# A windowed-attention and expert-attention kernel rewritten: block transposes on VectorE, packed TensorE tiles, expert pairs woven into the next batch

## The chip, the cores and the metric

One Trainium2 chip, one core of it. The metric is the time of one execution in device microseconds (us), the median of several runs. A core has TensorE (PE in the profile; its weight loads are PEld), VectorE (DVE), ScalarE (ACT), GpSimd (POOL) and SyncE (SP), which here only issues transfers.

## The reference, cut to what matters

```python
# q, k, v: (8 batches, 8 heads, 576, 64), float32
scores = matmul(q, k.T) / 8;  mask = abs(i - j) <= 32     # windowed attention
attn = exp(scores - max) * mask; attn /= attn.sum(-1)
x = (attn @ v) as (8, 576, 512)                           # heads side by side
logits = x @ w_gate                                       # 4 experts, the best 2 kept, softmax of the 2
for e in range(4):
    q, k, v = x @ wq[e], x @ wk[e], x @ wv[e]             # 512 -> 64
    a = softmax(causal(q @ k.T / 8))                      # 576 x 576
    out += weight[e] * (a @ v @ wo[e])                    # 64 -> 512
```

The largest score is not subtracted in either kernel; the inputs are small.

## The kernel before, in words

All loops are unrolled when the program is built, and a scheduler of the framework orders each engine's instructions by priority (the order of the source) and readiness; waits and buffers follow from tiles and pools.

For each batch the windowed attention goes head by head. `stage_qk_dma` (L126) loads q (SP queue) and k (ACT queue) in blocks of 128 positions; `stage_qk_compute` (L146) transposes each block for two heads on TensorE (L151) and ACT (L155) and DVE (L157) copy the results out. `head_stage1` (L165) loads v beside a column block of ones (L169, L171), makes the scores of five key blocks, each against the queries that its band reaches (L188, 832 columns a head, contraction over the 64 features of the head), lets ACT take the exponential (L193, L195, L200) and POOL multiply by the band mask (L202, L208, L210). `head_stage2` (L215) multiplies by v and the ones (L230), adds the overlapping edges of the blocks (L240 to L245), takes the reciprocal of 64x576 sums on DVE (L248) and multiplies (L249) into `XTF`, x transposed. Every float32 matmul shows in the trace as two load-and-multiply pairs.

`moe_batch` (L252) casts x to bfloat16 (L255), makes the gate in float32 (L262) and its top-2 weights on DVE, projects (L310, L321), and then goes through four experts one after the other: scores of one key block (L339), exponential (L361), triangle mask on DVE (L363), product with v and ones (L368), reciprocal and weight per block of queries (L390 to L394), transposes (L399). Last come the output projection with a contraction over 64 (L407), the copy (L410) and the store (L411). PSUM is a rotation of 8 single banks.

The order of the source is heads(0), then for each b: heads(b+1), moe(b). The loads for batch b+2 are issued among the heads of b.

Of the kernel before, what the change touches and what calls it, by code (L numbers as in the profile page):

```python
# [8 lines left out]
F32 = mybir.dt.float32  # L10
# [4 lines left out]
SUB = mybir.AluOpType.subtract  # L15
IS_GE = mybir.AluOpType.is_ge
AXX = mybir.AxisListType.X


@with_exitstack  # L20
def kernel(
# [12 lines left out]
    nc = tc.nc  # L34
    B, H, S, D = q.shape
    assert D == 64
    E, DM, HD = moe_wq.shape
    assert HD == 64 and DM == H * D and E == 4
    assert S % 128 == 64 and S == 576, "kernel tuned for S=576"
    W = 32  # L40
# [4 lines left out]
    NTB = (S + 127) // 128  # L45
    NKB = NTB
    NQT = NTB
    NKT = NTB

    kblocks = []  # L50
    for kb in range(NKB):
        k0 = 128 * kb
        nk = min(128, S - k0)
        q_lo = max(0, k0 - W)
        q_hi = min(S, k0 + nk + W)
        kblocks.append((k0, nk, q_lo, q_hi - q_lo))
    at_off = []
    acc = 0
    for (_, _, _, qw) in kblocks:
        at_off.append(acc)  # L60
        acc += qw
    ATW = acc

    consts = ctx.enter_context(tc.tile_pool(name="consts", bufs=1))
    wpool = ctx.enter_context(tc.tile_pool(name="wpool", bufs=1))
    stage = ctx.enter_context(tc.tile_pool(name="stage", bufs=1))
    natp = ctx.enter_context(tc.tile_pool(name="natp", bufs=12))
    qkt = ctx.enter_context(tc.tile_pool(name="qkt", bufs=3))
    vwp = ctx.enter_context(tc.tile_pool(name="vwp", bufs=3))
    atp = ctx.enter_context(tc.tile_pool(name="atp", bufs=3))  # L70
    xwp = ctx.enter_context(tc.tile_pool(name="xwp", bufs=2))
    xtp = ctx.enter_context(tc.tile_pool(name="xtp", bufs=2))
    mpool = ctx.enter_context(tc.tile_pool(name="mpool", bufs=2))
    smallp = ctx.enter_context(tc.tile_pool(name="smallp", bufs=2))
    psum = ctx.enter_context(tc.tile_pool(name="psum", bufs=1, space=bass.MemoryType.PSUM))

    def psum_b1(name):
        return psum.tile([128, 512], F32, name=name, tag="B1", bufs=8)
# [5 lines left out]
    BMK = consts.tile([128, 192], F32, name="BMK")  # L84
    nc.vector.memset(BMK, 1.0)
    nc.gpsimd.affine_select(BMK, BMK, pattern=[[1, 192]], compare_op=IS_GE, fill=0.0,
                            base=0, channel_multiplier=-1)
    nc.gpsimd.affine_select(BMK, BMK, pattern=[[-1, 192]], compare_op=IS_GE, fill=0.0,
                            base=64, channel_multiplier=1)
    QW0 = kblocks[0][3]  # L90
    BMK0 = consts.tile([128, QW0], F32, name="BMK0")
    nc.vector.memset(BMK0, 1.0)
    nc.gpsimd.affine_select(BMK0, BMK0, pattern=[[1, QW0]], compare_op=IS_GE, fill=0.0,
                            base=32, channel_multiplier=-1)
    nc.gpsimd.affine_select(BMK0, BMK0, pattern=[[-1, QW0]], compare_op=IS_GE, fill=0.0,
                            base=32, channel_multiplier=1)
    MT = consts.tile([128, 128], BF16, name="MT")
    nc.vector.memset(MT, 1.0)
    nc.gpsimd.affine_select(MT, MT, pattern=[[1, 128]], compare_op=IS_GE, fill=0.0,
                            base=0, channel_multiplier=-1)  # L100

    WG = wpool.tile([128, NDT, 4], F32, name="WG")
    nc.sync.dma_start(WG[:, :, :], moe_w_gate.rearrange("(t p) e -> p t e", p=128))
    WQP = [wpool.tile([128, NDT, 128], BF16, name=f"WQP{j}") for j in range(2)]
    WKP = [wpool.tile([128, NDT, 128], BF16, name=f"WKP{j}") for j in range(2)]
    WV = wpool.tile([128, NDT, 4 * 64], BF16, name="WV")
    WO = wpool.tile([64, E, DM], BF16, name="WO")
# [368 lines left out]
```

## Time and profile before

| what | us |
|---|---|
| timed runs | 916.01, 922.34, 925.95 |
| median | 922.34 |
| span of the profiled execution, first to last instruction | 916.9 |
| TensorE / VectorE / ScalarE / GpSimd busy in it | 744.7 / 504.8 / 317.1 / 174.6 |

The profiled execution is known by its span alone; what lies around the span is not in its record. Busy shares are means over the whole span; matmul ends are modelled, so neighbouring matmuls overlap in their records. PEclk is the granted TensorE clock in tenths or as a fraction of 2.4 GHz: the two levels are 1.0 (2.4 GHz) and 0.5 (1.2 GHz).

### The profile page before, as it was taken

The page shows a single profiled execution, that of the slowest core. Times are in us where ns is not written, and L with a number is a line of the kernel's source. Part 1 is how long each engine was busy: PE and PEld are TensorE (multiplying, and loading weights), DVE is VectorE, ACT ScalarE, POOL GpSimd, SP SyncE. Part 2 cuts the span into 40 slices and gives each one's busy share as a digit, 9 for nine tenths or more (in the row PEclk, how much of TensorE's full clock was granted, in tenths as well). Part 3 has the DMA queues.
Part 4 walks back from the last instruction along what each step waited for, and adds up shares of the span by engine and source line. Part 5 has one row for each costly group of instructions (what it writes and reads, how often), then busy time and mean ns, then how long its engine had stood idle before and what let it go on. Part 6 is the DMA issues. An engine that isn't in the chain of part 4 may idle for free.

```text
span 916.9 us, 10477 instructions
## 1 busy us (share of the span) xinstructions
PE 744.7 (81%) x3328; PEld 482.0 (53%) x3328; DVE 504.8 (55%) x1410; ACT 317.1 (35%) x1009; POOL 174.6 (19%) x267
## 2 busy tenths in 40 slices
PE   1798967859898598976979679895899679974997
PEld 1576735524675256743558435672467435852552
DVE  2328567672556716477174761658608960598242
ACT  1334333333423324233243233432424333333243
POOL 1044511001520014200242002420036002500000
PEclk9998656755757557575576755776559655776575
DMA  9936123001330013200141001110012001100001
GB/s 180 196 77 134 28 51 72 20 0 47 73 69 20 0 46 86 63 13 1 46 94 39 7 0 46 26 33 0 1 51 49 4 1 46 39 1 1 35 18 53
DMA packets 126407, 40.54 MB, mean 44 GB/s; under 512 B 121488, under 2 KB 121488, under 8 KB 126352
## 3 DMA queue, kind: packets, MB, share of 16 engines
q1 hardware_dynamic: 83728, 29.38, 13.7%
q10 hardware_dynamic: 42624, 10.49, 6.0%
q8 instruction: 27, 0.44, 0.2%
q14 instruction: 28, 0.23, 0.1%
HBM read 30.42 MB, written 9.44 MB: 43 GB/s over the span
## 4 chain that ended last, share of the span: by engine, by line
PE 66%; DVE 23%; DMA 4%; ACT 3%; issue 2%; ACTq 1%; SPq 0%; DVEq 0%
DVE REC L248 15%; PE pSB L188 10%; PE pOB L230 9%; PE py L407 8%; PE po L368 7%; PE pOA L230 7%; PE pSA L188 7%; PE pst L339 6%; PE pg L262 4%; PE pp L310 4%; PE ptt L399 3%; DVE XTF L249 3%; PE ptq L151 2%; DMA nat<-in_k_dram 2%; DVE XW L243 2%
## 5 line engine op out<-in xcount | busy, mean ns | idle before, releaser
L248 DVE RECIPROCAL REC<-XW 64x576 f32<-64x576 f32 x64 | 239.9, 3748 | 10.9 <-ACT XW L245 8.9
L368 PE MATMUL po<-VE,ATE 128*128 128x65 bf16 (+2 forms) x480 | 79.6, 245 | 69.5 <-DVE ATE L363 39.4
L151 PE MATMUL ptq<-ident,nat 128*128 128x128 f32 (+1 forms) x320 | 77.9, 376 | 62.2 <-DMA nat<-in_q_dram 18.5
L202 POOL TENSOR_TENSOR ATK<-ATK,BMK 128x160 f32<-128x160 f32 x64 | 34.3, 536 | 429.4 <-ACT ATK L193 428.4
L368 PEld LDWEIGHTS <-ATE 128*128 128x128 bf16 (+2 forms) x480 | 43.9, 117 | 126.0 <-ACT XTB L255 40.7
L188 PE MATMUL pSB<-QT,KT 64*128 64x192 f32 (+1 forms) x384 | 103.5, 404 | 2.4 <-ACT ATK L193 2.4
L230 PE MATMUL pOB<-ATK,VWK 128*128 128x192 f32 (+1 forms) x384 | 100.2, 392 | 0.8 <-ACT XW L245 0.8
L361 ACT ACTIVATE ATE<-pst 128x512 bf16<-128x512 f32 (+2 forms) x192 | 70.3, 390 | 85.9 <-PE pst L339 64.0
L208 POOL TENSOR_TENSOR ATK<-ATK,BMK 128x576 f32<-128x576 f32 x64 | 89.7, 1402 | 48.2 <-ACT ATK L195 45.7
L151 PEld LDWEIGHTS ptq<-ident,nat 128*128 128x128 f32 (+1 forms) x320 | 48.4, 183 | 91.3 <-DVE KT L157 25.2
L243 DVE TENSOR_TENSOR XW<-XW,pOA 128x64 f32<-128x64 f32 x64 | 14.0, 219 | 147.2 <-ACT XW L240 146.5
L188 PEld LDWEIGHTS pSB<-QT,KT 64*128 64x128 f32 (+1 forms) x384 | 80.3, 235 | 26.3 <-issue 22.0
L230 PEld LDWEIGHTS pOB<-ATK,VWK 128*128 128x128 f32 (+1 forms) x384 | 82.5, 242 | 21.2 <-issue 12.7
L243 DVE TENSOR_TENSOR XW<-XW,pOB 128x64 f32<-128x64 f32 x192 | 41.4, 220 | 94.1 <-ACT XW L245 86.7
L188 PE MATMUL pSA<-QT,KT 64*128 64x160 f32 (+1 forms) x256 | 78.9, 447 | 0.0
L407 PE MATMUL py<-WO,OTT 64*128 64x512 bf16 (+1 forms) x160 | 77.5, 623 | 0.0
L230 PE MATMUL pOA<-ATK,VWK 128*128 128x160 f32 (+1 forms) x256 | 73.0, 420 | 4.3 <-issue 1.4
L339 PE MATMUL pst<-QE,KE 64*128 64x512 bf16 (+2 forms) x192 | 69.1, 387 | 2.3 <-ACT ATE L361 2.3
L245 ACT COPY XW<-pOB 128x128 f32<-128x128 f32 (+1 forms) x192 | 45.2, 242 | 72.5 <-DVE XW L243 51.4
L390 DVE RECIPROCAL rr<-po 128x1 f32<-128x1 f32 (+1 forms) x160 | 26.3, 165 | 64.3 <-PE po L368 63.9
L193 ACT ACTIVATE ATK<-pSA 128x352 f32<-128x352 f32 x64 | 29.7, 465 | 84.1 <-PE pSA L188 76.7
L188 PEld LDWEIGHTS pSA<-QT,KT 64*128 64x128 f32 x256 | 54.4, 268 | 8.4 <-issue 8.2
(70 smaller groups left out, 858.3 us busy)
## 6 DMA issues: line engine op xcount, KB each, us to landing
nat<-in_k_dram ACTq DMA_DIRECT2D x32, 256.0 KB, 4.5
nat<-in_q_dram SPq DMA_DIRECT2D x32, 256.0 KB, 4.3
VWK<-in_v_dram SPq DMA_DIRECT2D x64, 128.0 KB, 2.3
out_dram<-ysb SPq DMA_DIRECT2D x32, 256.0 KB, 2.0
VWK<-in_v_dram ACTq DMA_DIRECT2D x64, 16.0 KB, 2.4
nat<-in_q_dram SPq DMA_DIRECT2D x8, 128.0 KB, 3.0
nat<-in_k_dram ACTq DMA_DIRECT2D x8, 128.0 KB, 3.7
out_dram<-ysb SPq DMA_DIRECT2D x8, 128.0 KB, 2.3
```

Of the source, the lines that this page charges most:

```text
L151: nc.tensor.transpose(pt[:, 0:nt], nat[:nt, 2 * g:2 * g + 2, :].rearrange("p h d -> p (h d)"), ident[:nt, :nt])
L188: nc.tensor.matmul(tgt[0:nk, col:col + qw], KTl[g][pofs:pofs + 64, k0:k0 + nk], QTl[g][pofs:pofs + 64, q_lo:q_lo + qw], start=True, stop=True)
L208: nc.gpsimd.tensor_tensor(out=a13, in0=a13, in1=BMK[:, None, 0:iw].to_broadcast([128, 3, iw]), op=MULT)
L230: nc.tensor.matmul(tgt[:, col:col + qw], VWK[0:nk, kb, :], ATK[0:nk, at_off[kb]:at_off[kb] + qw], start=True, stop=True)
L243: nc.vector.tensor_tensor(out=XW[:, q_lo:prev_hi], in0=XW[:, q_lo:prev_hi], in1=tgt[:, col:col + ovl], op=ADD)
L245: nc.scalar.copy(XW[:, prev_hi:q_hi], tgt[:, col + ovl:col + qw])
L248: nc.vector.reciprocal(REC[0:64, :], XW[64:128, :])
L262: nc.tensor.matmul(pg[0:nt, 4 * tb:4 * tb + 4], XTF[dt][:, t0:t0 + nt], WG[:, dt, :], start=(dt == 0), stop=(dt == NDT - 1))
L339: nc.tensor.matmul(pst[0:nkk, 0:cw], KE[jj2][eo2:eo2 + 64, k0:k0 + nkk], QE[jj2][eo2:eo2 + 64, k0 + c:k0 + c + cw], start=True, stop=True)
L361: nc.scalar.activation(ATE[0:nkk, c:c + cw], pst[0:nkk, 0:cw], EXP, scale=scale_moe)
L368: nc.tensor.matmul(po[qt][0:nq, 0:65], ATE[0:nkk, q0 - k0:q0 - k0 + nq], VE[kt][0:nkk, e, 0:65], start=(kt == 0), stop=(kt == qt))
L407: nc.tensor.matmul(py[0:nq, 0:DM], OTT[:, e, q0:q0 + nq], WO[:, e, :], start=(e == 0), stop=(e == E - 1))
```

## The change

Nearly everything is rewritten; inputs, outputs and types (float32 for the windowed part and the gate, bfloat16 for the experts) stay. The windowed attention takes 4 heads at a time (g = 0, 1). q and k of four heads are loaded so that each head fills 32 partitions, and four VectorE transposes of 32x32 blocks (two halves of the 64 features each for q and k) replace the TensorE transposes. Each score matmul contracts over 32 partitions into 64 partitions of PSUM, and the two feature halves accumulate: a head, a feature half and the parity of the 64-wide key block give a part of the array of its own. The sums of the four heads come from matmuls with one-hot columns into 32 partitions each, 128x144 in all, and one reciprocal serves them. v multiplies in segments whose 128 keys cover the band of the segment, so nothing is added at edges; the reciprocals are spread over partitions by a matmul with a selector (`rb`). v is loaded once for a batch, and two SBUF-to-SBUF transfers make the blocks that begin at odd multiples of 64.

The experts go in pairs: scores of both into one two-bank tile, one exponential for up to 1024 elements of a partition, triangle masks by POOL, one set of normalizing instructions per pair, and the output projection contracts over both experts (128). PSUM is 4 slots of two banks. Of batch b-1, gate, projections and scores stand among the heads of batch b. All transfers but the weights go through the SP queue, q and k of the first batch first.

```diff
-    (stage_qk_dma, stage_qk_compute, head_stage1, head_stage2, moe_batch)
+    natp bufs=3; qkt, vp, xp, mp, atep bufs=2; atp, yp bufs=3; psum bufs=4 of [128, 2, 512] f32
+    def load_qk(b, g):
+        for nm, src in (("qn", q), ("kn", k)):
+            t = natp.tile([128, 18, 64], F32, name=nm, tag=nm)
+            for hh in range(4):
+                nc.sync.dma_start(t[32 * hh:32 * hh + 32, :, :],
+                                  src[b, 4 * g + hh].rearrange("(tb p) d -> p tb d", p=32))
+    def load_v(b):
+        t = vp.tile([128, 8, H, 64], F32, name="vsb", tag="vsb")
...
+        pairs = t[:, :, :, :].rearrange("p (m o) h d -> p m o (h d)", o=2)
+        nc.sync.dma_start(pairs[64:128, :, 1, :], pairs[64:128, :, 0, :])
+        nc.sync.dma_start(pairs[0:64, 0:3, 1, :], pairs[0:64, 1:4, 0, :])
+    EBLK = [[(0, 0, 96), (1, 96, 224), (2, 224, 288)], [(2, 288, 352), (3, 352, 480), (4, 480, 576)]]
+    OBLK = [[(0, 0, 160), (1, 160, 288)], [(2, 288, 416), (3, 416, 576)]]
+    SEGS = [(0, 96), (96, 160), (160, 224), (224, 288), (288, 352), (352, 416), (416, 480), (480, 576)]
+    def win_scores(b, g):
+        for T, nm in ((KT, "kn"), (QT, "qn")):
+            for dh in range(2):
+                nc.vector.transpose(T[:, dh, :].rearrange("p (t x) -> p t x", x=32),
+                                    n_[:, :, 32 * dh:32 * dh + 32])
+        for half in range(2):
+            sl = [slot("sc0"), slot("sc1")]
+            with tc.manual_schedule(engines={PE}):
+                for s in range(3):
+                    for dh in range(2):
+                        for par, blk in ((0, eb), (1, ob)):
...
+                            for hh in range(4):
+                                r = slice(32 * hh, 32 * hh + 32)
+                                nc.tensor.matmul(
+                                    sl[hh // 2][64 * par:64 * par + 64, hh % 2, lo - c0:hi - c0],
+                                    KT[r, dh, k0:k0 + 64], QT[r, dh, lo:hi],
+                                    start=(dh == 0), stop=(dh == 1), skip_group_check=True)
+            for p in range(2):
+                nc.scalar.activation(ap, sl[p][:, :, 0:HS], EXP, scale=scale_att)
+                nc.gpsimd.tensor_tensor(out=ap, in0=ap, in1=MASK[...], op=MULT)   # 128 x 576
+    def win_out(b, g):
+        ss = slot("sums")
+        for hh in range(4):
+            for j in range(4):
+                nc.tensor.matmul(ss[32 * j:32 * j + 32, 0, 0:144], OH[:, hh, :],
+                                 A[:, hh, 144 * j:144 * j + 144], ...)
+        nc.vector.reciprocal(R, ss[:, 0, 0:144])
+        for pair in range(2):
+                for c, (lo, hi) in enumerate(SEGS):
+                    for x in range(2):
+                        nc.tensor.matmul(up_[64 * x:64 * x + 64, half, ...], V[:, c, 4 * g + hh, :], A[:, hh, lo:hi], ...)
+        for pair in range(2):
+            nc.scalar.copy(us, u[pair][:, :, 0:HS])
+            for j in range(4):
+                nc.tensor.matmul(rb[...144 columns], SEL[:, j, pair, :], R, start=True, stop=True)
+            nc.vector.tensor_tensor(out=XTF[...], in0=us, in1=rb[:, :, 0:HS], op=MULT)
+            nc.gpsimd.tensor_copy(XTB[:, dt, :], XTF[:, dt, :])
+    moe_scores(b, j): 12 matmuls of the two experts j, 4 exponentials (3 of 1024, 1 of 128 elements), 4 affine_select on POOL
+    moe_av(b, j): 30 matmuls, 2 x (reciprocal, weight, scale), 5 transposes of both experts, 1 copy
+    moe_y(b): 10 matmuls of 512 columns, copies of 1024 on DVE, ACT, DVE, 3 stores
+    load_weights()
+    for b in range(B + 1):
+        for g in range(2):
+            if b + 1 < B:
+                load_qk(b + 1, g)
+                if g == 0:
+                    load_v(b + 1)
+            if b < B:
+                win_scores(b, g)
+            if b > 0:
+                if g == 0:
+                    moe_gate(b - 1); moe_proj_qk(b - 1, 0); moe_scores(b - 1, 0); moe_proj_v(b - 1)
+                else:
+                    moe_av(b - 1, 0)
+            if b < B:
+                win_out(b, g)
+            if b > 0:
+                if g == 0:
+                    moe_proj_qk(b - 1, 1); moe_scores(b - 1, 1)
+                else:
+                    moe_av(b - 1, 1); moe_y(b - 1)
```

## Rows read from the trace of the kernel before

**Rows 1.** The page: busy time of each engine, and the granted clock by slice.
```profile
PE 744.7 (81%) x3328; PEld 482.0 (53%) x3328; DVE 504.8 (55%) x1410; ACT 317.1 (35%) x1009; POOL 174.6 (19%) x267
...
PEclk9998656755757557575576755776559655776575
```
**Rows 2.** Stretches: the first 60 us, and one batch period of 113 us.
```profile
core 0: us, PE busy (x) PEld busy (x) DVE busy (x) ACT busy (x) POOL busy (x), PEclk, DMA share, GB/s
0.00:60.00 60.00, 35.28 (x133) 27.62 (x134) 16.08 (x65) 15.58 (x56) 7.88 (x21) 1.00 0.98 167
368.00:481.00 113.00, 94.05 (x417) 60.87 (x417) 61.78 (x177) 39.34 (x126) 21.35 (x32) 0.62 0.18 42
```
**Rows 3.** The page: the chain that ended last, shares by engine.
```profile
PE 66%; DVE 23%; DMA 4%; ACT 3%; issue 2%; ACTq 1%; SPq 0%; DVEq 0%
```
**Rows 4.** That chain in order of time, within 505 to 536 us: time, length, what.
```profile
514.83 3.75 DVE REC L248
...
526.86 3.75 DVE REC L248
```
**Rows 5.** Groups by shape: operation, count | busy us, mean ns | idle before.
```profile
L248 DVE RECIPROCAL REC<-XW 64x576 f32<-64x576 f32 x64 | 239.9, 3748 | 10.9 <-ACT XW L245 8.9
L208 POOL TENSOR_TENSOR ATK<-ATK,BMK 128x576 f32<-128x576 f32 x64 | 89.7, 1402 | 48.2 <-ACT ATK L195 45.7 <-ACT XW L245 1.6
...
L249 DVE TENSOR_TENSOR XTF<-XW,REC 64x576 f32<-64x576 f32 x64 | 51.3, 802 | 1.2
...
L195 ACT ACTIVATE ATK<-pSB 128x384 f32<-128x384 f32 x64 | 31.5, 492 | 51.1 <-PE pSB L188 50.9
...
L361 ACT ACTIVATE ATE<-pst 128x512 bf16<-128x512 f32 x32 | 19.1, 597 | 25.7 <-PE po L368 13.5 <-PE pst L339 12.2
```
**Rows 6.** Timeline of PE, 556 to 582 us, low clock: start, length, work.
```profile
556.46 5.86 PE L407 MATMUL py<-WO,OTT 64*128 64x512 bf16 x13
562.25 1.54 PE L188 MATMUL pSA<-QT,KT 64*128 64x160 f32 x4
...
565.51 1.54 PE L188 MATMUL pSA<-QT,KT 64*128 64x160 f32 x4
```
**Rows 7.** Timeline of PE, 580 to 584 us, high clock.
```profile
581.16 0.79 PE L188 MATMUL pSA<-QT,KT 64*128 64x160 f32 x4
...
582.83 0.86 PE L230 MATMUL pOA<-ATK,VWK 128*128 128x160 f32 x4
```
**Rows 8.** Timeline of PEld at 55.7 and 799.4 us: first and last of 24.
```profile
55.74 0.28 PEld L230 LDWEIGHTS pOB<-ATK,VWK 64*128 64x128 f32 x1 [0.44 <-issue]
55.74 0.28 PEld L188 LDWEIGHTS pSA<-QT,KT 64*128 64x128 f32 x1
...
799.39 0.18 PEld L230 LDWEIGHTS pOB<-ATK,VWK 64*128 64x128 f32 x1 [0.23 <-issue]
799.39 0.18 PEld L188 LDWEIGHTS pSA<-QT,KT 64*128 64x128 f32 x1
```
**Rows 9.** Timeline of PE, the gate of one batch, high clock.
```profile
164.61 4.91 PE L262 MATMUL pg<-WG,XTF 128*128 128x4 f32 x40
169.45 0.61 PE L310 MATMUL pp<-XTB,WQP 128*128 128x512 bf16 x1
```
**Rows 10.** Timeline of PE, small expert matmuls, low clock.
```profile
321.94 0.82 PE L368 MATMUL po<-VE,ATE 128*128 128x65 bf16 x7
322.69 0.31 PE L399 MATMUL ptt<-ident_bf,OEs 128*64 128x128 bf16 x1
```
**Rows 11.** Groups by shape, PEld: the load after a change of array shape.
```profile
L188 PEld LDWEIGHTS pSB<-QT,KT 64*64 64x64 f32 x128 | 15.4, 170 | 22.0 <-issue 22.0
```
**Rows 12.** Timeline of POOL, start of the program.
```profile
1.59 0.35 POOL L86 TENSOR_SCALAR_AFFINE_SELECT BMK<-BMK 128x192 f32<-128x192 f32 x1
...
2.75 0.31 POOL L99 TENSOR_SCALAR_AFFINE_SELECT MT<-MT 128x128 bf16<-128x128 bf16 x1
```
**Rows 13.** The page: transfers by issue, KB each, us to landing.
```profile
nat<-in_q_dram SPq DMA_DIRECT2D x32, 256.0 KB, 4.3
```
**Rows 14.** Timeline, 0 to 30 us: the first work of PE.
```profile
16.82 1.94 PE L151 MATMUL ptq<-ident,nat 128*128 128x128 f32 x8 [16.82 <-DMA nat<-in_q_dram]
```

More of the change, by code (lines that the diff above doesn't have):

```diff
@@ L15 @@
 SUB = mybir.AluOpType.subtract
+MAX = mybir.AluOpType.max
 IS_GE = mybir.AluOpType.is_ge
+NEQ = mybir.AluOpType.not_equal
 AXX = mybir.AxisListType.X
+PE = mybir.EngineType.PE
+S = 576
+HS = 288
 @with_exitstack
@@ L34 @@
     nc = tc.nc
-    B, H, S, D = q.shape
-    assert D == 64
+    B, H, S_, D = q.shape
     E, DM, HD = moe_wq.shape
-    assert HD == 64 and DM == H * D and E == 4
-    assert S % 128 == 64 and S == 576, "kernel tuned for S=576"
-    W = 32
+    assert S_ == S and D == 64 and H == 8 and HD == 64 and DM == 512 and E == 4
     scale_att = 1.0 / (D ** 0.5)
@@ L80 @@
+    load_qk(0, 0)
+    load_v(0)
+    load_qk(0, 1)
     ident = consts.tile([128, 128], F32, name="ident")
@@ L261, in moe_batch, with off, moe_gate @@
+    def off(kt, c):
+        if kt == 0:
+            return c if c < 512 else 960 + c - 512
+        return {1: 512 + c - 128, 2: 1024 + c - 256, 3: 1344 + c - 384, 4: 1536 + c - 512}[kt]
+    CHUNKS = [[(0, 0, 512, 0)], [(1, 128, 576, 0), (0, 512, 576, 448)],
+              [(2, 256, 576, 0), (3, 384, 576, 320)], [(4, 512, 576, 0)]]
+    st = {}
+    def moe_gate(b):
+        XTF = xtf.pop((b, "F"))
+        pg = slot("pg")
+        for t in range(NQT):
+            n = nrow(t)
             for dt in range(NDT):
-                nc.tensor.matmul(pg[0:nt, 4 * tb:4 * tb + 4],
-                                 XTF[dt][:, t0:t0 + nt],
-                                 WG[:, dt, :],
+                nc.tensor.matmul(pg[0:n, 0, 4 * t:4 * t + 4], XTF[:, dt, 128 * t:128 * t + n], WG[:, dt, :],
@@ new lines, in moe_y @@
+    def moe_y(b):
+        OTT = st.pop(("OTT", b))
+        for t0 in (0, 2, 4):
+            py = slot("py")
+            tiles = [t for t in (t0, t0 + 1) if t < NQT]
+            for t in tiles:
+                n = nrow(t)
+                for j in range(2):
+                    nc.tensor.matmul(py[0:n, t - t0, :], OTT[:, j, 128 * t:128 * t + n], WO[:, j, :],
+                                     start=(j == 0), stop=(j == 1))
+            ysb = yp.tile([128, 2, DM], F32, name="ysb", tag="ysb")
+            n = nrow(t0)
+            m = len(tiles)
+            if t0 == 2:
+                nc.scalar.copy(ysb[0:n, 0:m, :], py[0:n, 0:m, :])
+            else:
+                nc.vector.tensor_copy(ysb[0:n, 0:m, :], py[0:n, 0:m, :])
+            if m == 2:
+                nc.sync.dma_start(out[b, 128 * t0:128 * t0 + 256, :].rearrange("(a p) d -> p a d", p=128), ysb)
+            else:
+                nc.sync.dma_start(out[b, 512:576, :], ysb[0:64, 0, :])
@@ new lines @@
+    load_weights()
[9 more added lines that the diff above has]
+                if g == 0:
+                    moe_gate(b - 1)
+                    moe_proj_qk(b - 1, 0)
+                    moe_scores(b - 1, 0)
+                    moe_proj_v(b - 1)
+                else:
+                    moe_av(b - 1, 0)
[3 more added lines that the diff above has]
+                if g == 0:
+                    moe_proj_qk(b - 1, 1)
+                    moe_scores(b - 1, 1)
+                else:
+                    moe_av(b - 1, 1)
+                    moe_y(b - 1)
```

586 lines of the change are left out of this document (227 added, 359 removed).

## The prediction

> **What bounds the kernel now.** I read the page first. TensorE is busy for 81% of the span, yet its clock is mostly at or near the low level [rows 1]: it is the nearest thing to a bound, running at about six tenths of its speed. A table of stretches comes next, because the program repeats itself: the loads of a batch recur every 113 us, and in such a period PE is busy for 94.05 us at a mean clock of 0.62 while VectorE is busy for 61.78, ScalarE for 39.34 and GpSimd for 21.35 [rows 2]. So 19 us of a period are PE's idle time. The chain that ended last says whose fault they are: 66% PE, 23% DVE [rows 3], and in order of time it is the reciprocal of 64x576 sums, 3.75 us each, behind which the small gate and expert instructions of DVE queue while PE waits [rows 4]. 64 of them cost 239.9 us [rows 5].
>
> So two things are to be priced: how much work for PE the new program has, and what else could take a period's end.
>
> **A measure of PE's work, tried on the old program.** A float32 matmul of N columns is two load-and-multiply pairs, 2N record columns. A head's five score matmuls make 2 x 832 = 1664. At the low clock one head follows the other after 565.51 - 562.25 = 3.26 us [rows 6], 1.96 ns a column; at the high clock the same ten pairs take 582.83 - 581.16 = 1.67 us [rows 7], 1.00 ns. For bfloat16, 13 matmuls of 512 columns take 562.25 - 556.46 = 5.79 us at the low clock [rows 6], 0.87 ns a column, so about 0.435 at the high one. The gate is bound by its 40 loads: 169.45 - 164.61 = 4.84 us at the high clock [rows 9]. Small expert matmuls take (322.69 - 321.94)/7 = 0.107 us at the low clock [rows 10], about 0.054 at the high one. The old period in high-clock time is then: 16 head passes x 1.67 = 26.7; 40 block transposes (9216 record columns) 9.2; gate 4.8; 30976 bfloat16 columns (projections 14336, scores 6400, output 10240) 13.5; 80 small ones 4.3: together 58.5. Divided by the clock of 0.62 this is 94.4 us, and the row says 94.05. The measure holds, so I use it for the new program, with the same clock.
>
> **The new windowed part.** Per four heads the scores are 80 matmuls, 9216 columns, 18432 record columns. Taken singly they cost more than before, since a contraction over 32 rows costs as many columns as one over 64 and there are two halves. All hangs on whether matmuls on different parts of the array run at once. The trace shows it for row halves: where the last block of a head (rows 0 to 63) is followed by the scores of an odd head (rows 64 to 127), the two loads begin together and each lasts as long as the other, 0.18 us at the high clock and 0.28 at the low one, so neither holds the other up; 24 such meetings, of which the first and the last are shown [rows 8]. For column halves no row exists: the bounds are one after the other and fully side by side. I take side by side, as the nearest row is this one, two matmuls on disjoint parts of the array. With four row groups and two column halves at once, only the widest block of each wave counts: 160+128+64 in one half of the queries, 128+160+96 with the wider of each pair in the other (736), times two feature halves, times two records, 2944 record columns, 2.9 us. (Rows alone side by side: 18432/4, 4.6 us; nothing: 18.4 us.) Sums: 16 matmuls of 144 columns, 4608 record columns, four column groups: 1.15 us (4.6 one by one). Products with v: 2304 columns, 4608 record columns in two column halves: 2.3 us (4.6). Spreading the reciprocals: 8 x 144, 2304 record columns over the whole array: 2.3 us. Sum 8.7 us for four heads, 17.4 for a batch; 32.3 if only row groups overlap; 59.9 if nothing does. It replaces 26.7 + 9.2 = 35.9.
>
> The Trainium skill, "TensorE: Matmul & The Clock Gate", Part 3, gives 2.38 as the measured gain of three column tiles; an estimate with a gain of about 1.6 for two and 3.1 for four would put the windowed part near 19 us a batch instead of 17.4, some 3 us more in a period. No run shows it yet.
>
> **The expert part.** Gate 4.8. Projections 14336 and output 5120 columns (half of before, as it contracts over both experts) 8.5. Scores 6400 columns, alternating between the row halves, so 3200 at the measure of the meetings: 1.4. 70 small ones 3.8. Sum 18.5, against 22.6 before (58.5 - 35.9).
>
> **Changes of array shape.** The new program moves between 32x64, 128x32, 128x64, 64x128 and 128x128, some 20 times a batch. In the old one the last score block (64x64) comes behind 64x128 ones, and the load unit idles 22.0 us over the 64 heads with no releaser, 0.34 us each [rows 11]; part of this is only the previous matmul streaming, so the cost lies between 0 and 0.34. I take 0.1: 2 us a batch, at most 7. The Trainium skill, "TensorEngine Tiling (Array Packing)", Key Properties, says that a change of tiling mode drains the engine: this speaks against the change, and the idle row agrees in kind. By that rule with the whole 0.34 the period would be 8 us longer.
>
> PE's work in a period is thus 17.4 + 18.5 + 2 = 37.9 us at the high clock, 61 us at 0.62.
>
> **The other engines in a period.** DVE: eight block transposes of 576 elements. No row shows one; the bounds are the plain 64x576 product at 0.80 and the reciprocal at 3.75 us [rows 5]; I take 0.8, a plain stream of as many elements, 6.4 together (30 at the upper bound). Two reciprocals of 144 elements, 3748 x 144/576 = 0.94 each; four products 3.2; gate, copies and normalizing some 11: 22 us, against 61.78. With the upper bound 46, still under 61. ACT: twelve instructions of 576 elements at about 0.65 (between 0.49 for 384 and the slope to 0.60 for 512 [rows 5]), six of 1024 at 1.1, others 3: 17 us. POOL: eight masks of 576 at 1.40 [rows 5], 11.2; eight selects of 128 to 384 elements at 0.31 to 0.55 [rows 12], 3.5; four casts of 576, between 0.35 and 1.40, taken as 0.9, 3.6: 18 us. Transfers: 4.7 MB as before plus 0.9 MB inside SBUF; the first 60 us moved 167 GB/s [rows 2], so 34 us. None reaches 61, so each is hidden as long as the order lets it be; the loads of a batch are issued a period ahead of use, and a block of 256 KB lands in 4.3 us [rows 13]. If SP, which now issues the stores and waits in order, delayed a load of 2.4 MB, up to 14 us of a period would show.
>
> What becomes late next is hand-over. Four masks of POOL take 5.6 us behind the scores, and `win_out` waits for them. In the first half of a batch gate, projections and scores of experts (about 9 us at the high clock) stand in that place. In the second only `moe_av` does, 2 to 3 us, so some idle time is left there, and the exponentials of 1024 elements (1.1 us) hold the four PSUM slots. I set 5 us a period (0 to 15) in place of the old 19.
>
> **The sum.** A period is 61 + 5 = 66 us; seven full ones make 462. Before them come the first loads and a batch without experts: PE started at 16.8 us, behind the weights [rows 14]; now q and k of four heads (1.2 MB, 7 us at 167 GB/s) come first, but v, the other heads, weights and prefetch share the transfers, so I put 30 us until the second period. Behind them one batch of experts alone, 18.5 us at the low clock: 37, and 3 for the last store. 30 + 462 + 37 + 3 = 532 us of span. The old span of 916.9 stands 5 us under the median of 922.34, so the forecast is 537, rounded to 535.
>
> **The rivals.**
> 1. *PE comes to the high clock more often.* With fewer waits for DVE the clock could be 0.85: 37.9/0.85 + 5 = 50; 30 + 350 + 30 + 3 + 5 = 418 us. For it: the high level comes inside a dense float32 stretch [rows 7], and the new program is such work for longer. Against: the 20 us before, just as dense, run at the low level [rows 6], with no wait at all.
> 2. *The clock stays low, or the hand-overs cost 20 us:* 37.9/0.5 + 5 = 81; 30 + 567 + 37 + 3 + 5 = 642 us. For it: tiny matmuls in short bursts; a period near 0.5 is seen in several slices [rows 1].
> 3. *Only row groups overlap:* 32.3 + 18.5 + 2 = 52.8, at 0.62 85 + 5 = 90; 30 + 630 + 37 + 3 + 5 = 705 us. For it: no row shows column halves together.
> 4. *Slower: the packed matmuls take turns,* because the load and the two passes of each keep the array. 59.9 + 18.5 + 2 = 80.4, at 0.62 130 + 5 = 135; 30 + 945 + 37 + 3 + 5 = 1020 us. It decides from a period of (922 - 75)/7 = 121 us on, which is 72 us of PE work at the high clock, where overlap saves less than 9 of the 60 us of the windowed part. Against it stand the 24 meetings.
>
> **How the numbers follow.** Forecast 0.46, by itself 470 to 600; rival 1 0.20, rival 2 0.17, rival 3 0.10, rival 4 0.06; 0.01 for something near no change. The range from 410 to 700 holds the forecast, rivals 1 and 2 and half of rival 3. Faster by over 1% (about what a measurement of this kernel can tell from no change): the first four, 0.93; within 1%: 0.01; slower: 0.06.
>
> **What would show it.** Right: periods near 66 us; PE leading the chain with DVE under a tenth; DVE about 180 us busy in all; score matmuls of four heads starting within a few ns of each other, a wave of 40 in 2 us or less at the high clock; a block transpose of 0.6 to 1 us. Wrong: score records that follow one another by their full streaming time; a chain led by POOL's masks or by transfers; a clock under 0.55 or over 0.8; periods over 80 us.

## The result and the profile after

The changed kernel takes 488.86 us (median of 4 runs, 483.65 to 491.71) where the kernel before took 922.06 beside it on the same chip: the ratio is 0.526, with a 95% interval of 0.522 to 0.530. The forecast was 535 us. The profiled execution took 491.21 us, its span 489.5. Ratios here are of undisturbed runs; in others a kernel was granted a few hundredths less clock and took some per cent longer (this profiled execution is one: 0.815, against 0.823 in the run of 483.65 us), so a ratio can lie a little below that of the medians.

The page of the changed kernel, first the engines' busy time and the granted clock in 40 slices, then the chain that ended last:

```profile
PE 367.7 (75%) x5920; PEld 281.2 (57%) x5920; DVE 195.6 (40%) x385; ACT 129.0 (26%) x194; POOL 142.4 (29%) x194
...
PEclk9978879877997759976599765979799776989576
...
PE 56%; DVE 14%; DMA 10%; SPq 9%; issue 5%; ACT 2%; POOL 1%; ACTq 1%; DVEq 0%
```

Beside [rows 1] and [rows 3]: PE's busy time is halved (744.7 to 367.7 us), VectorE's falls from 504.8 to 195.6 us, and the clock is mostly at 7 to 9 tenths where it was at 5 to 7. VectorE's share of the chain falls from 23% to 14%, and what is left is no longer the reciprocal: the small product `rg` (L379) and the block transposes (L177) have some 22 us each. Transfers rise from 4% to 10% of the chain and SP's queue from nothing to 9%. Of these 94 us, 36 lie before the first gate and 46 more before 140 us; behind that only two loads of k, of 5.5 and 5.8 us, are left.

The program repeats itself once a batch, and the gate (L262) marks where. The stretches from gate to gate; columns are the length, busy time of PE, PEld, DVE, ACT and POOL, the granted clock, the busy share of the DMA engines and GB/s:

```profile
0.00:59.60 59.60, 28.94 (x705) 23.53 (x705) 18.06 (x29) 10.78 (x16) 21.71 (x41) 0.89 1.12 179
59.60:114.80 55.20, 43.85 (x743) 33.42 (x741) 22.39 (x47) 15.75 (x25) 16.88 (x22) 0.85 0.68 115
114.80:170.80 56.00, 44.74 (x742) 34.45 (x740) 25.24 (x47) 15.91 (x25) 17.65 (x22) 0.83 0.58 105
170.80:231.90 61.10, 47.56 (x745) 36.70 (x741) 25.16 (x47) 16.02 (x25) 18.42 (x23) 0.78 0.57 101
231.90:292.20 60.30, 47.66 (x741) 36.66 (x740) 23.80 (x47) 16.30 (x25) 17.30 (x22) 0.78 0.49 92
292.20:348.50 56.30, 44.95 (x741) 35.45 (x740) 23.87 (x47) 15.30 (x23) 14.83 (x20) 0.80 0.48 96
348.50:403.30 54.80, 43.70 (x744) 33.44 (x740) 24.20 (x47) 15.84 (x24) 16.84 (x22) 0.84 0.51 101
403.30:451.90 48.60, 39.52 (x583) 29.66 (x580) 21.14 (x41) 13.80 (x22) 15.58 (x20) 0.85 0.01 2
451.90:489.50 37.60, 26.80 (x197) 17.90 (x196) 11.76 (x34) 9.26 (x13) 3.19 (x8) 0.68 0.18 63
```

So the span is a start of 59.6 us, seven periods of 392.3 us together (56.0 each, where 113 stood in [rows 2]; the last one, of 48.6, holds the scores of four heads less than the others) and a tail of 37.6 us. PE's idle time in a period is its length less the first busy column: 11.35 us in the first, 13.5 in the third. The clock goes with the length: 0.85 in the shortest, 0.78 in the two longest. The clock of the first stretch says little: up to 24.95 us the record has no entry, and the profile shows that as 1.00, though the first scores of four heads took 4.63 us there and 2.90 at 56.77. The same holds for the 1.00 of the first 60 us in [rows 2].

One high-clock stretch of a period on PE (start, length, work) is the measure of each stage:

```profile
246.07 2.46 PE L324 MATMUL pv<-WV,XTB 128*128 128x256 bf16 x20 [0.59 <-ACT ATE L347]
248.46 1.19 PE L212 MATMUL sums<-AT,OH 128*32 128x144 f32 x32
249.58 2.28 PE L226 MATMUL u<-AT,vsb 128*64 128x96 f32 x64
251.79 2.23 PE L238 MATMUL rb<-R,SEL 128*128 128x144 f32 x16
...
256.83 0.97 PE L344 MATMUL ps<-QKE 64*128 64x512 bf16 x12 [0.85 <-DVE QKE L312]
258.92 2.59 PE L194 MATMUL sc<-QT,KT 32*64 32x96 f32 x128 [1.12 <-DVE KT L177]
```

Sums 1.19 us (1.15 was worked out), products with v 2.28 (2.3), spread reciprocals 2.23 (2.3). The scores of four heads are cut by a wait here (128 of 160 records); whole ones took 2.90 us at 56.77 (a row further down), where 2.9 was worked out. In the trace the first matmuls of the four heads start there 6 to 7 ns apart. Between sums, products and spreads the array's shape changes twice (128x32, 128x64, 128x128), and each begins where the one before ends.

### The profile page after: what moved, and what is told of

The parts are those of the page before. It is cut to its first block, busy times and chain, and to the rows that moved or that the text cites. A ratio compares the mean times of both kernels' runs of the same rounds, so it can differ in the third digit from the quotient of the medians.

```text
span 489.5 us, 13183 instructions
## 1 busy us (share of the span) xinstructions
PE 367.7 (75%) x5920; PEld 281.2 (57%) x5920; DVE 195.6 (40%) x385; ACT 129.0 (26%) x194; POOL 142.4 (29%) x194
## 2 busy tenths in 40 slices
DMA packets 129352, 48.04 MB, mean 98 GB/s; under 512 B 120848, under 2 KB 120848, under 8 KB 129296
## 4 chain that ended last, share of the span: by engine, by line
PE 56%; DVE 14%; DMA 10%; SPq 9%; issue 5%; ACT 2%; POOL 1%; ACTq 1%; DVEq 0%
PE sc L194 9%; PE pg L262 8%; PE pp L305 6%; PE u L226 6%; SPq L76 6%; PE po L372 5%; PE py L399 5%; PE sums L212 5%; PE rb L238 5%; DVE rg L379 5%; PE pv L324 3%; DMA vsb<-in_v_dram 3%; SPq L84 2%; DMA kn<-in_k_dram 2%; DVE OE L381 2%
## 5 line engine op out<-in xcount | busy, mean ns | idle before, releaser
L201 POOL TENSOR_TENSOR AT<-AT,MASK 128x576 f32<-128x576 f32 x64 | 87.7, 1399 | 79.9 <-ACT AT L200 79.9
L194 PE MATMUL sc<-QT,KT 32*64 32x128 f32 (+3 forms) x2560 | 56.3, 307 | 49.0 <-DVE KT L177 42.5
L194 PEld LDWEIGHTS sc<-QT,KT 32*64 32x64 f32 x2560 | 47.8, 153 | 54.9 <-DVE KT L177 22.9
L347 ACT ACTIVATE ATE<-ps 128x1024 bf16<-128x1024 f32 x64 | 48.0, 836 | 32.8 <-PE ps L344 32.8
L262 PEld LDWEIGHTS pg<-WG,XTF 128*128 128x128 f32 (+1 forms) x320 | 49.1, 251 | 4.2 <-issue 3.5
L200 ACT ACTIVATE AT<-sc 128x576 f32<-128x576 f32 x64 | 38.2, 648 | 47.1 <-PE sc L194 47.0
L262 PE MATMUL pg<-WG,XTF 128*128 128x4 f32 (+1 forms) x320 | 49.9, 291 | 0.5 <-issue 0.5
L226 PE MATMUL u<-AT,vsb 128*64 128x64 f32 (+1 forms) x1024 | 44.3, 253 | 0.6 <-POOL AT L201 0.5
L226 PEld LDWEIGHTS u<-AT,vsb 128*64 128x64 f32 x1024 | 40.5, 159 | 6.8 <-issue 5.9
L241 DVE TENSOR_TENSOR XTF<-us,rb 128x576 f32<-128x576 f32 x32 | 24.1, 754 | 43.8 <-PE rb L238 37.6
L238 PE MATMUL rb<-R,SEL 128*128 128x144 f32 x256 | 37.6, 302 | 1.3 <-DVE R L216 1.3
L372 PE MATMUL po<-VE,ATE 128*128 128x65 bf16 (+2 forms) x480 | 28.3, 202 | 3.8 <-issue 3.2
```

The source lines that it names most:

```text
L194: nc.tensor.matmul(sl[hh // 2][64 * par:64 * par + 64, hh % 2, lo - c0:hi - c0], KT[r, dh, k0:k0 + 64], QT[r, dh, lo:hi], start=(dh == 0), ...
L200: nc.scalar.activation(ap, sl[p][:, :, 0:HS], EXP, scale=scale_att)
L201: nc.gpsimd.tensor_tensor(out=ap, in0=ap, in1=MASK[:, None, c0:c0 + HS].to_broadcast([128, 2, HS]), op=MULT)
L226: nc.tensor.matmul(up_[64 * x:64 * x + 64, half, lo - HS * half:hi - HS * half], V[:, c, 4 * g + hh, :], A[:, hh, lo:hi], start=True, stop ...
L238: nc.tensor.matmul(rb[:, j // 2, 144 * (j % 2):144 * (j % 2) + 144], SEL[:, j, pair, :], R, start=True, stop=True)
L262: nc.tensor.matmul(pg[0:n, 0, 4 * t:4 * t + 4], XTF[:, dt, 128 * t:128 * t + n], WG[:, dt, :], start=(dt == 0), stop=(dt == NDT - 1))
```

## The experiments

Ratios are to the kernel before; the change has 0.526. Unless said otherwise each edit below is of the changed kernel, and PE's idle time is summed from 58 to 420 us of the span.

**A product of 8 columns that waits for GpSimd.** The largest wait in a period is PE's for the experts' normalized output. A part of the timeline, all engines:

```profile
200.65 5.47 POOL L201 TENSOR_TENSOR AT<-AT,MASK 128x576 f32<-128x576 f32 x4
202.30 0.21 DVE L378 RECIPROCAL rg<-po 128x8 f32<-128x8 f32 x1 [4.10 <-PE po L372]
202.54 3.60 DVE L379 TENSOR_TENSOR rg<-rg,G 128x8 f32<-128x8 f32 x1
206.18 0.69 DVE L381 TENSOR_TENSOR OE<-po,rg 128x512 bf16<-128x512 f32 x1
...
206.93 0.61 PE L387 MATMUL pt<-ident_bf,OE 128*128 128x128 bf16 x4 [4.66 <-DVE OE L381]
```

The product of 128x8 takes 3.60 us, and ends as the fourth of GpSimd's masks does (200.65 + 5.47 = 206.12). Both its inputs lie in SBUF. The edit leaves the reciprocal in PSUM, so that only one does:

```diff
-            nc.vector.reciprocal(rg[0:n, :, t0:t1], pv_[0:n, :, t0:t1, 64])
-            nc.vector.tensor_tensor(out=rg[0:n, :, t0:t1], in0=rg[0:n, :, t0:t1],
+            nc.vector.reciprocal(pv_[0:n, :, t0:t1, 64], pv_[0:n, :, t0:t1, 64])
+            nc.vector.tensor_tensor(out=rg[0:n, :, t0:t1], in0=pv_[0:n, :, t0:t1, 64],
```

> The changed kernel, with the reciprocal of the expert sums left in PSUM, so that the small product rg (L379 of the changed kernel) has one operand in PSUM and one in SBUF instead of two in SBUF. Theory A (the product waits for GpSimd's masks because both read SBUF through something shared: its 128x8 form lasts 3.60 us where four masks of 5.47 us in a row end within 0.1 us of it): its mean falls from 1382 ns to about 0.2 us, PE's longest wait for OE falls from 4.7 to about 1.2 us, a period shrinks by 2.5 to 4 us, the time from 489 to 460 to 472 us. Theory B (the product is late for another reason, such as G in bfloat16 with a stride): the mean stays over 1 us and the time within 1%. Theory C (another wait takes the place at once, since the sums of the windowed part need the same masks): the mean falls, the time stays within 1%.

It took 465.19 us, ratio 0.499 (0.494 to 0.503), 24 us less than the change. The groups by shape, first of the changed kernel, then of this one (count | busy us, mean ns):

```profile
L379 DVE TENSOR_TENSOR rg<-rg,G 128x8 f32<-128x8 f32 x16 | 22.1, 1382 | 0.6
```
```profile
L379 DVE TENSOR_TENSOR rg<-po,G 128x8 f32<-128x8 f32 x16 | 2.7, 167 | 0.5
```

From 1382 to 167 ns, with the same masks on GpSimd beside it: the wait is for GpSimd, and an input in PSUM avoids it. From 58 to 420 us PE's waits for the normalized output fall from 30.8 to 17.7 us, its whole idle time only from 72.2 to 64.1; the rest of the gain goes with the clock, which is 0.87 in this window where it was 0.81. The Trainium skill, "SBUF — State Buffer", section "SBUF: two separate sides", says that a VectorE instruction with two SBUF inputs and a GpSimd instruction reading SBUF exclude each other, and that the one that starts first keeps the port for its whole length. The trace agrees that the product ends with a mask: all seven times that it met one in the changed kernel it ended within 0.03 us of a mask's end. It also shows more: here the product came during the second of four masks and ended only with the fourth, as it did in two other periods. That is no rule, though. In the kernel with VectorE's order by hand, further down, the product ends with the third of four masks while the fourth still runs:

```profile
193.20 5.47 POOL L208 TENSOR_TENSOR AT<-AT,MASK 128x576 f32<-128x576 f32 x4 [0.52 <-ACT AT L207]
...
196.01 1.33 DVE L386 TENSOR_TENSOR rg<-rg,G 128x8 f32<-128x8 f32 x1
```

Why it is held for one mask there and for up to three here, no run shows.

**Does the array take neighbours side by side?** The forecast rested on column halves and row groups overlapping, of which the trace of before showed only the row halves [rows 8]. Two kernels issue the same matmuls in an order in which neighbours lie on the same part: the scores one head after another (the loop over `hh` moved outermost), and the products with v head by head (`for x` moved outside `for c`).

```diff
-                for s in range(3):
-                    for dh in range(2):
...
-                            for hh in range(4):
-                                r = slice(32 * hh, 32 * hh + 32)
+                for hh in range(4):
+                    r = slice(32 * hh, 32 * hh + 32)
+                    for s in range(3):
```

> The changed kernel, with the score matmuls of one head in a row (10 in each half of the queries, alternating between the column halves) before those of the next head, instead of the four heads in turn. Theory A (row groups overlap only where they stand next to each other): 18432 record columns at two at once, about 9 us instead of 2.6 to 3.0 at the high clock for four heads, 16 times: some 100 us more at the high clock, 590 to 620 us. Theory B (the engine looks some tens of instructions ahead, so that the next head starts while the last still runs): between 3 and 6 us, 495 to 540 us.

604.61 us, ratio 0.654 (0.651 to 0.658). PE's timeline there:

```profile
208.31 11.96 PE L194 MATMUL sc<-QT,KT 32*64 32x96 f32 x160 [1.70 <-DVE KT L177]
```

11.96 us for 160 records, where the changed kernel took 2.90. Part of that is the clock; so here are the stretch of this kernel and one of the changed kernel at nearly as low a clock:

```profile
208.31:220.25 11.94, 11.86 (x161) 11.33 (x161) 0.51 (x1) 1.95 (x3) 4.20 (x3) 0.56 1.25 226
```
```profile
40.85:44.91 4.06, 4.02 (x160) 3.44 (x160) 0.52 (x1) 1.19 (x2) 1.36 (x1) 0.64 1.20 175
```

4.06 us at 0.64 would be 4.6 at 0.56, and 2.90 at 1.00 would be 5.2, so the order alone costs a factor of 2.3 to 2.6. What packs the array is the order of issue as much as the shape. The length fits neither theory: 11.96 us at 0.56 are 6.7 at the high clock, under theory A's 9 and above theory B's 3 to 6, so heads still overlapped in part. That the time fell into theory A's range even so goes with the clock, 0.71 over the run against 0.82, which theory A had not counted.

> The changed kernel, with the matmuls with v ordered head by head instead of alternating between the two heads of a pair, that is 16 matmuls in a row on one column half, then 16 on the other. Theory A (column halves overlap only where matmuls of both stand next to each other in PE's order): the products of four heads take about 4.6 us instead of 2.28 at the high clock, 16 times, so 37 us more work at the high clock and 525 to 540 us in all. Theory B (the engine looks far ahead, so that order does not matter): 2.3 us and 489 us within 1%.

497.65 us, ratio 0.538. Its products took 3.65 us where 2.28 stood, not the 4.6 of one by one: some neighbours still overlapped. The 1.4 us by 16 would be 22 us, but the time rose by 9, where theory A expected 36 or more. From 58 to 420 us PE was busy 11.5 us longer (301.29 against 289.79) and idle as much less, at a clock of 0.83 against 0.81: part of the longer work took the place of waits, and part is hidden by the clock.

**Loads in long rows, and the order of VectorE.** In the changed kernel K's transposes are done just before the scores that need them: PE waits 1.12 us before the scores at 258.92 above, and 22.5 us in all from 58 to 420 us. One edit read q and k in rows of 4608 bytes (the transposes then write with a stride):

```diff
-                                  src[b, 4 * g + hh].rearrange("(tb p) d -> p tb d", p=32))
+                                  src[b, 4 * g + hh].rearrange("(p tb) d -> p tb d", p=32))
-                nc.vector.transpose(T[:, dh, :].rearrange("p (t x) -> p t x", x=32),
+                nc.vector.transpose(T[:, dh, :].rearrange("p (x t) -> p t x", t=18),
```

> The changed kernel, with q and k loaded so that a partition takes 18 positions in a row, 4608 bytes at once instead of 18 pieces of 256, and the block transposes writing with a stride of 18 elements. Theory A (the first 57 us are bound by the number of pieces: 175 to 199 GB/s in pieces of 256 bytes): the transfers speed up, the gate of the first batch starts 12 to 25 us earlier than at 59.6 us, and as the periods stay near 56 us the time falls to 464 to 477 us. Theory B (bound by bytes or by what SP waits for): the gate starts within 4 us of before and the time stays within 1%. Theory C (the strided writes make the transposes slower): a transpose takes over 1.5 us instead of 0.74, and a part or all of the gain is lost.

461.07 us, ratio 0.498 (458.45 to 462.28 us). The DMA packets fell from 129352 to 59720, and yet the first gate started at 59.3 us: the start is not bound by the number of pieces, and there theory B was right, though not in its time. The gain lies in the periods. The transposes rose from 743 to 1232 ns, but VectorE now did K's well ahead of the scores, and PE's idle time before scores fell from 22.5 to 7.9 us. Was it the rows or the order? A first try moved the transposes in the source only:

> The VectorE transposes of q and k for the next four heads are issued one step earlier, before this step's masks and copies; the loads stay in short rows. Theory A (the gain of the run with long rows, 461 us, came from K's transposes standing ahead of the scores on VectorE): PE's idle time before scores falls from 22.5 us (58 to 420 us) to under 9, and the time is 462 to 472 us. Rival B (the gain came from the long rows themselves): idle before the scores stays near 22, time within 1% of 488.9.

488.19 us, ratio 0.528. This settles nothing: VectorE's instructions stood in the same order as before. The framework's scheduler had put them back; why it did so is not shown. So the order was then written by hand, with the loads left in short rows:

```diff
+                with tc.manual_schedule(engines={DVE}):
+                    if b < B:
+                        win_tr(b, 1)
+                    if b > 0:
+                        moe_proj_qk(b - 1, 1)
...
+                with tc.manual_schedule(engines={DVE}):
+                    if b + 1 < B:
+                        win_tr(b + 1, 0)
+                    if b > 0:
+                        moe_av(b - 1, 1)
```

> VectorE's order is now written by hand where it matters: the transposes of the next four heads stand ahead of the last q/k copy of the step before and ahead of the second half of the experts' output (in the run before, the edit in the source left that order as it was). Loads stay in short rows. Theory A (K's late transposes cost what the run with long rows gained): PE's idle time before scores falls from 22.5 us (58 to 420 us) to under 10, time 462 to 475 us. Rival B (the gain was of the long rows): time within 1% of 488.9 although the transposes come early.

459.92 us (455.18 to 476.10), ratio 0.493 (0.491 to 0.495): as much as the long rows gave. The idle time before scores fell to 11.1 us, a little above the 10 that was expected. But PE's whole idle time hardly fell (72.2 to 71.1 us), it went to other waits. The window 58 to 420 us of the changed kernel, and then of this one (columns as above):

```profile
58.00:420.00 362.00, 289.79 (x4687) 223.10 (x4676) 149.15 (x298) 101.30 (x154) 108.20 (x134) 0.81 0.53 97
```
```profile
58.00:420.00 362.00, 290.94 (x5196) 226.18 (x5197) 156.45 (x327) 110.58 (x168) 118.60 (x146) 0.90 0.54 98
```

PE is as busy (290 us) and does more in it (5196 records against 4687): the gain is the clock, 0.90 instead of 0.81. The gate shows it best. PE's timeline up to the gate, in the changed kernel and in this one:

```profile
225.07 3.38 PE L194 MATMUL sc<-QT,KT 32*64 32x96 f32 x134 [1.55 <-DVE KT L177]
230.72 1.22 PE L194 MATMUL sc<-QT,KT 32*64 32x128 f32 x26 [2.28 <-issue]
231.88 7.94 PE L262 MATMUL pg<-WG,XTF 128*128 128x4 f32 x40
```
```profile
213.71 2.62 PE L201 MATMUL sc<-QT,KT 32*64 32x96 f32 x160
216.26 4.29 PE L269 MATMUL pg<-WG,XTF 128*128 128x4 f32 x40
```

and the granted clock in the stretches around them (last but two of the columns):

```profile
221.00:231.00 10.00, 6.13 (x153) 3.52 (x159) 3.25 (x4) 2.20 (x3) 2.76 (x2) 0.67 0.72 180
231.00:241.00 10.00, 10.00 (x72) 9.29 (x64) 1.01 (x8) 1.41 (x3) 2.76 (x2) 0.50 1.02 189
```
```profile
216.00:226.00 10.00, 9.15 (x90) 6.91 (x74) 2.95 (x14) 2.77 (x6) 5.42 (x4) 0.83 0.96 199
```

In the changed kernel the scores come in pieces between waits (PE busy 6.13 of 10 us), and the gate behind them runs at the low level, in 7.94 us where [rows 9] had 4.91. In this one the scores come whole and the gate takes 4.29. Waits of nearly the same total cost less where they lie now. The pair shown is the clearest: three of the changed kernel's eight gates took 7.9 us and the others 4.9 to 5.8, while five of this one's took 4.29 and one 7.30. Elsewhere in the period this kernel has low stretches too (the scores at 190.09 took 4.04 us at 0.60).

**What held the clock before.** The kernel before, with its reciprocal and product replaced by one multiplication:

```diff
-        nc.vector.reciprocal(REC[0:64, :], XW[64:128, :])
-        nc.vector.tensor_tensor(out=XTF[g][pofs:pofs + 64, :],
-                                in0=XW[0:64, :], in1=REC[0:64, :], op=MULT)
+        nc.vector.tensor_scalar_mul(out=XTF[g][pofs:pofs + 64, :], in0=XW[0:64, :],
+                                    scalar1=1.0 / 65.0)
```

> The kernel before, with its reciprocal and product per head replaced by one multiplication with a constant; the division by the sums of the attention is left out, nothing else. It asks what holds the granted clock of the kernel before at .62. Theory A (PE's short waits for VectorE after each head): with the 240 us of reciprocals gone the clock rises to .75 or more, the period of 113 us falls to about 75 (94 us of PE work at .62 is 73 at .80), in all 600 to 690 us. Rival B (the kind of PE's work, 4-byte matmuls on half or a quarter of the array): clock .58 to .68, PE bound at 94 us a period, 760 to 820 us.

702.12 us, ratio 0.760 (0.757 to 0.764): 219 us less than before, where the whole change gained 433. The time lies between what the two theories expected; the clock, 0.76 from 58 to 420 us and 0.738 in all, about reaches theory A's 0.75. The kernel before, and this one:

```profile
58.00:420.00 362.00, 291.06 (x1282) 195.09 (x1282) 220.63 (x507) 125.17 (x424) 81.36 (x121) 0.65 0.21 48
```
```profile
58.00:420.00 362.00, 348.13 (x1844) 233.59 (x1843) 150.77 (x727) 171.82 (x587) 105.28 (x158) 0.76 0.27 63
```

Here PE's idle time falls from 70.9 to 13.9 us and the clock rises from 0.65 to 0.76. But the sum of the waits does not set it: the changed kernel has as much idle time in this window (72.2 us) as the kernel before (70.9), at 0.81. And PE's work without waits can be at the low level too: in the kernel with the scores head by head the window read

```profile
58.00:420.00 362.00, 322.90 (x3797) 269.43 (x3787) 109.64 (x238) 81.56 (x121) 88.16 (x108) 0.69 0.43 78
...
220.20:230.00 9.80, 9.80 (x51) 9.05 (x50) 1.50 (x11) 0.87 (x2) 1.40 (x1) 0.50 0.78 163
```

with the gate, behind 11.82 us of scores without a gap, again at 0.50. The clock fell within those scores: it was 0.97 in their first 1.5 us and 0.56 over all of them. So low stretches are seen behind crowded waits and behind long dense work; what decides in general stays open.

**The start.** Weights issued by SP, behind the first batch's loads, instead of by ACT beside them:

```diff
-        nc.scalar.dma_start(WG[:, :, :], moe_w_gate.rearrange("(t p) e -> p t e", p=128))
+        nc.sync.dma_start(WG[:, :, :], moe_w_gate.rearrange("(t p) e -> p t e", p=128))
...
```

> The weight loads are issued by SP, behind the first batch's q, k and v, instead of by ACT beside them. Theory A (the first gate starts at 59.6 us, where 30 was forecast, because the weights' bytes share the DMA engines with the second half of k, which lands at 38.6): k's second half lands by 30, the first gate starts at 47 to 51, and the run takes 476 to 481 us. Rival B (the start is set by the order on PE and by the sum of bytes, so that moving the weights only moves the wait): first gate at 57 or later, time within 1% of the changed kernel's 488.9.

485.06 us, ratio 0.526 (0.522 to 0.529): no difference that can be measured. The first scores of the second half and of the second batch, and the gate, in the changed kernel and in this one:

```profile
40.85 4.05 PE L194 MATMUL sc<-QT,KT 32*64 32x96 f32 x160 [3.63 <-DVE KT L177]
56.77 2.90 PE L194 MATMUL sc<-QT,KT 32*64 32x96 f32 x160 [1.70 <-DVE KT L177]
59.59 2.62 PE L262 MATMUL pg<-WG,XTF 128*128 128x4 f32 x22
```
```profile
31.61 4.20 PE L194 MATMUL sc<-QT,KT 32*64 32x96 f32 x160 [3.62 <-DVE KT L177]
51.09 2.90 PE L194 MATMUL sc<-QT,KT 32*64 32x96 f32 x160 [3.01 <-DVE KT L177]
53.92 3.61 PE L262 MATMUL pg<-WG,XTF 128*128 128x4 f32 x27
```

The second half's k comes 9 us earlier and the gate 5.7 us, less than expected, and of that too little remains to be measured: here the rival's time came, by another course.

**Together.** The three edits with the transposes moved in the source only:

> Three edits together: the reciprocal of the routing left in PSUM, weights behind the first batch's loads, transposes one step ahead. If the gains add (24 us from the first, about 10 and 20 from the others) the time is 430 to 445 us, the granted clock .85 or more. Rival: they cover for one another, because PE is the bound once one wait is gone: 455 to 465 us.

459.94 us, ratio 0.491 (0.487 to 0.496), in the rival's range. With the order by hand:

> The transposes' order, the routing's reciprocal left in PSUM and the weights behind the first batch's loads, together. If they take away separate waits (20, 24 and 5 us): 438 to 448 us, PE's idle time in 58 to 420 us under 45 (from 72.2). Rival (they cover for one another, the next wait in line ends as late): 455 us or more, idle over 55.

456.74 us, ratio 0.495 (0.493 to 0.497). The rival was right: after the order alone (0.493) the other two edits add nothing. The wait for GpSimd is partly gone there already: the product still meets the masks, but is held for one of them at most (its mean over both shapes is 420 ns, 769 in the changed kernel). And the order by hand makes waits of its own. It puts four transposes ahead of the second half of the experts' output, and PE now waits 3.13 us for that, where it waited 1.24 with the routing's reciprocal edited alone:

```profile
202.46 1.43 DVE L180 STREAM_TRANSPOSE KT<-kn 128x576 f32<-128x576 f32 x2
...
203.81 1.40 DVE L180 STREAM_TRANSPOSE QT<-qn 128x576 f32<-128x576 f32 x2
...
206.30 0.61 PE L394 MATMUL pt<-ident_bf,OE 128*128 128x128 bf16 x4 [3.13 <-DVE OE L388]
```

PE's idle time from 58 to 420 us is 65.6 us, over the rival's 55, and the clock is 0.84 where the order alone had 0.90. With the long rows as well, and then with the first gate and projections ahead of the second batch's scores:

> The same three and the long rows of 4608 bytes (half the DMA packets, transposes written with a stride at 1.23 us instead of 0.74). Theory A (long rows themselves give nothing once the order is right): within 1% of the run with three edits. Rival B (shorter transfers count): faster by over 2%. Rival C (64 longer transposes, 31 us of VectorE, count): slower by over 2%.

443.37 us, ratio 0.479 (0.476 to 0.482), 3.3% less than with three edits. By its time theory B, but VectorE's and PE's orders changed with it, so that the rows alone are not shown to be the cause. Against the change this version is 9% faster.

> The four edits, and the first batch's gate and its first projections moved ahead of the second batch's scores on PE. Theory A (the first gate, at 54 us in the run with the weights moved, waits only because the scores of batch 1 stand ahead of it in order and their k lands at 46): first gate at 38 to 44 us and the time 6 to 12 us below the run with four edits. Rival B (the bytes bound the start: about 10 MB in the first 57 us): the gate starts earlier but the second period grows by as much, time within 1%.

441.82 us, ratio 0.477 (0.475 to 0.479), the same within 1%: theory B. The gate starts at 46.2 instead of 54.8 us, and the next one at 111.0 instead of 108.4: the second batch's scores now wait in their turn:

```profile
59.11 4.37 PE L201 MATMUL sc<-QT,KT 32*64 32x96 f32 x131 [4.67 <-DVE QT L180]
```

## Why the prediction was right

The direction, the mechanism and the range held: PE's work is as packed as forecast, the waits for the reciprocal are gone, and 489 lies in the forecast's own 470 to 600. Three terms of the sum were off, and they partly cancel, so that the number came so near is in part luck: with the 30 us forecast for the start the time would have been about 459, below the forecast's own range. By its own signs the prediction was not right in all: the clock went over 0.8, which it had named as a sign of being wrong, the periods are 56 us and not near 66, and VectorE has 14% of the chain and not under a tenth.

- *PE's work for a period, 37.9 us at the high clock:* right. The first period has 43.85 us at 0.85, which is 37.3; the third 47.56 at 0.78, 37.1. Two errors cancel in it: the windowed part's stages come to 17.2 us a batch, so about 20 are left for the experts, where 18.5 were put, and the 2 for changes of shape are not seen. Each stage of the windowed part is within 0.1 us of its term. The heart of it, column halves side by side, was a choice between bounds; the runs with the order undone show that it was the packing. Rivals 3 and 4, which let column halves take turns, are out: four-fold sums in 1.19 us are 4608 columns at a quarter of 1.00 ns each. So is the weaker gain for column tiles that the figure of 2.38 for three in the Trainium skill ("TensorE: Matmul & The Clock Gate", Part 3) would have given: two gave 2.0 and four 3.9. The measure itself agreed with the old period in part by luck: it charges the old kernel's 40 transposes 9.2 us at the high clock, 14.8 at 0.62, and the trace has them busy for 9.14 us in that period, so other terms were too low. The new kernel has no such transposes.
- *Changes of array shape, 2 us:* the rows at 248 to 252 us show no gap at all. The drain of which the Trainium skill ("TensorEngine Tiling (Array Packing)", Key Properties) speaks is not to be seen at these two changes.
- *The clock, 0.62:* the term that was furthest off. It was carried over from the kernel before because the measure of PE's work had held with it; but it is no property of the work. It was 0.81 over the periods, near rival 1's 0.85. With 0.81 the forecast's own period is 37.9/0.81 + 5 = 52 us instead of 66. Part of the low clock before was due to the waits for the reciprocal, as the run without it shows.
- *Hand-over, 5 us a period:* 11 us, inside the bounds of 0 to 15, by waits that were not named: the experts' 8-column product behind GpSimd's masks, and K's transposes late in VectorE's order. GpSimd's masks were priced as a wait for `win_out`, not as something that holds VectorE. With both terms corrected a period is 47 + 11 = 58 us, against 56.0 measured (57.3 without the last one).
- *The start, 30 us:* 59.6. 179 GB/s were moved in it, near the 167 assumed, but about 10.7 MB (179 GB/s by 59.6 us) come before the gate, and the second batch's scores stand ahead of it. Of the first 140 us of the chain that ended last, 82 are transfers and their issue. The start takes back 30 of the 7 x 10 = 70 us that the periods are shorter. This, and the hand-overs, is why rival 1's clock came without its 418 us.
- *The tail, 40 us:* 37.6. *Span to median, 5:* the profiled execution lies 1.7 us above its span.
- VectorE's busy time was put at about 180 us, and is 195.6. A block transpose took 0.74 us (0.8 taken). The reciprocal left takes 1058 ns for 144 columns of 128 rows (0.94), and stands in the chain only once.

## What to carry to other kernels

Price the work of a packed array at the widest of its neighbours, and issue the neighbours next to each other: the same 80 matmuls took 2.3 to 2.6 times as long in another order at a like clock. Don't carry a mean granted clock from one program to another; look for the stretch at the low level and at what PE did just before it, since nearly the same total of waits went with 6% less time when they lay elsewhere in the period (0.493 against 0.526). Before splitting work between VectorE and GpSimd, look for VectorE instructions with both inputs in SBUF beside long GpSimd runs; and read the order on each engine from the trace, because the source need not give it.

## What the runs showed of the hardware

- A VectorE product of 128x8 took 3.60 us beside GpSimd's masks and 0.17 with one input in PSUM. With both in SBUF it ended with a mask each time that it met one in the changed kernel: the one in which it began, or one or two masks later.
- The same gate of 40 matmuls took 4.91 us [rows 9], 7.94 at the low level, or 4.29 (clock 1.0); the lengths went with what PE had done before. The clock fell to the low level behind waits, and also within 11.96 us of scores without a gap (0.97 in the first 1.5 us, 0.56 over all).
- Row groups and column groups of the array overlapped for float32 when neighbours in the order of issue lay on different ones: four column groups passed 4608 record columns in 1.19 us, four row groups with two column halves 18432 in 2.90.
- A 32x32 block transpose of 128x576 float32 took 743 ns with contiguous writes and 1232 ns with a stride of 18 elements.
